# An attention and two expert layers on one core: the durations of the list scheduler set to those of a trace

## The chip, the cores and the metric

The kernel runs on one core of a Trainium2 chip. A core has four engines that compute: TensorE (PE in the profile; PEld is its weight loading), VectorE (DVE), ScalarE (ACT) and GpSimd (POOL). Each takes its instructions strictly in the order in which the program lists them. SyncE (SP) issues every DMA transfer of this kernel, also in order. The metric is the device time of one execution in microseconds (us).

## The reference

An attention for 4 batches of 8 heads (576 positions of 64 values, 32 packed queries) feeds a dense expert layer, and that feeds eight routed experts:

```python
p_packed = softmax(p @ k.T * scale) @ v          # 32 packed rows per head
x = softmax(q @ p_packed.T * scale) @ p_packed   # 576 rows per head -> [2304, 512]
h = x @ w_in                                     # w_in [512, 2048], float64
x = (h * clip(h + 3, 0, 6) / 6) @ w_out          # first layer
P = exp(x @ w_gate - max); 8 times: rows, then columns of P to a fixed sum
out = sum over e of P[:, e] * (relu(x @ w1[e]) @ w2[e])   # second layer, e = 0..7
```

The operands of the large products are split exactly into a high and a low part of twelve significant bits, and three passes (high by high, high by low, low by high) are summed in PSUM.

## The kernel before, in words

The program is not written in the order in which it runs. Every operation (one DVE instruction, one group of matmuls, one DMA) is first recorded with the engines that may do it, an assumed duration, the tiles that it reads and writes, and a priority. `Order.run` (line 95) then simulates the engines: again and again it takes, of the operations whose inputs are ready in the simulation, the one that can start first, ties going to the priority, and emits it. So the assumed durations decide both the order on each engine and, for operations with two possible engines, which engine does them. `alt` (line 299) lets POOL or DVE do a subtraction of two tiles, and DVE gets it only where it would end earlier than POOL by more than a margin `spare`; `copy` (line 289) chooses between ACT and DVE. `SYNC = 0.2` is added between an operation and whatever depends on it. The DMA's assumed time (`dma`, line 286) is the larger of 0.6 us and KiB / 350, and 2 us to land.

The durations come from four functions (lines 134 to 147): `t_dve`, `t_act`, `t_pool` and `t_pe`, each a fixed part and a part per column.

The work falls into these stages. In the attention, eight units of four heads each load k, q and v (lines 480, 497, 505), transpose and multiply them on PE (lines 527 to 772) and write tiles `a2`. In the same stretch the first float64 weights (tiles `raw`, line 381) are decoded on ACT, DVE and POOL into `w1f` (line 337) and `w2`. Then comes the first layer: `packed_weights` (matmuls of line 810), `layer1a` (lines 848 to 850, 288 columns) and `layer2a` (lines 885 to 887), 32 blocks in all. `third_phase` then frees memory, `operands` prepares the tokens of a pair of blocks for Winograd's form of Strassen's product (additions of line 936; high parts `xyh` and low parts `xyl`, lines 417 and 422), and the routing's 8 rounds run in small DVE operations. In the second layer a unit is one pair of token blocks with one group of 256 hidden units: seven products of 384 columns (lines 958 to 960, into `ph`), sums on DVE (line 967), relu on ACT (line 973), the split into `hsh` (ACT, line 417) and `hsl` (POOL or DVE, line 422), and six products of 512 columns (lines 1007 to 1009, into `po`), which DVE adds to `acc` (line 1031). There are 32 units for the first pair (a new group of weights for each), then 64 for the other two.

## Time and profile before

| what | value |
|---|---|
| three runs | 1975.92, 1979.96, 1982.13 us (median 1979.96) |
| the profiled execution, first to last instruction | 1972.3 us |
| PE busy in it | 1922.3 us, 97% |
| DVE, POOL, ACT busy | 1392.9, 1052.1, 874.1 us |
| last transposition of the attention | starts at 127.42 us |
| first layer ends, second begins | about 453.6 us |
| mean granted clock of PE | 0.996 |

The profile gives the span of the profiled execution, and no other time of that execution; the median of the runs is 7.7 us above the span, the fastest run 3.6 us.

A busy PE here means that a matmul is in flight. Since they overlap, a matmul's own length (338 ns for 384 columns) is about twice the distance from one to the next; the pace is read from counts in a stretch.

### The profile page before, as it was taken

The page shows a single profiled execution, that of the slowest core. Times are in us where ns is not written, and L with a number is a line of the kernel's source. Part 1 is how long each engine was busy: PE and PEld are TensorE (multiplying, and loading weights), DVE is VectorE, ACT ScalarE, POOL GpSimd, SP SyncE. Part 2 cuts the span into 40 slices and gives each one's busy share as a digit, 9 for nine tenths or more (in the row PEclk, how much of TensorE's full clock was granted, in tenths as well). Part 3 has the DMA queues.
Part 4 walks back from the last instruction along what each step waited for, and adds up shares of the span by engine and source line. Part 5 has one row for each costly group of instructions (what it writes and reads, how often), then busy time and mean ns, then how long its engine had stood idle before and what let it go on. Part 6 is the DMA issues. An engine that isn't in the chain of part 4 may idle for free.

```text
span 1972.3 us, 29636 instructions
## 1 busy us (share of the span) xinstructions
PE 1922.3 (97%) x10957; PEld 1733.2 (88%) x10957; DVE 1392.9 (71%) x2499; ACT 874.1 (44%) x1992; POOL 1052.1 (53%) x1045
## 2 busy tenths in 40 slices
PE   6999999998999999999999999999999999999998
PEld 4789989997888999999889899999999999999997
DVE  6885686437988777777866767667676676767665
ACT  6885775435354444444453334333333333333332
POOL 2454575326787766677744445454454544545442
PEclk9999999999999999999999999999999999999999
DMA  9921121001212221222301111110111111111102
GB/s 212 199 78 33 54 65 44 12 1 32 65 57 67 70 74 66 65 66 74 88 31 43 33 33 34 32 44 33 33 33 33 43 33 33 33 33 43 33 11 65
DMA packets 103553, 104.95 MB, mean 53 GB/s; under 512 B 42736, under 2 KB 78576, under 8 KB 103408
## 3 DMA queue, kind: packets, MB, share of 16 engines
q1 hardware_dynamic: 103408, 103.06, 19.0%
q8 instruction: 86, 1.41, 0.3%
q14 instruction: 59, 0.48, 0.1%
HBM read 98.32 MB, written 4.72 MB: 52 GB/s over the span
## 4 chain that ended last, share of the span: by engine, by line
PE 71%; DVE 4%; issue 1%; ACT 0%; ACTq 0%; DVEq 0%
PE po L1009 13%; PE po L1007 13%; PE po L1008 13%; PE ph L958 11%; PE ph L960 11%; PE ph L959 11%; DVE acc L1025 1%; DVE acc L1019 1%; DVE tmp L936 1%; DVE tmp L967 1%; DVE acc L1031 0%; DVE hsl L422 0%; DVE xyl L422 0%; DVE w1xl L422 0%; ACT tmp L973 0%
## 5 line engine op out<-in xcount | busy, mean ns | idle before, releaser
L422 POOL TENSOR_TENSOR hsl<-tmp,hsh 128x384 fp32r<-128x384 f32 (+1 forms) x503 | 505.1, 1019 | 541.0 <-ACT hsh L417 538.4
L1031 DVE SCALAR_TENSOR_TENSOR acc<-po,Pr,acc 128x512 f32<-128x512 f32 x504 | 373.6, 748 | 186.2 <-PE po L1009 184.8
L967 DVE TENSOR_TENSOR tmp<-ph,tmp 128x384 f32<-128x384 f32 x672 | 364.1, 554 | 165.9 <-PE ph L960 150.3
L1009 PE MATMUL po<-w2h,hsl 128*128 128x512 f32 x1152 | 449.1, 390 | 2.8 <-DVE hsl L422 2.8
L1007 PE MATMUL po<-w2h,hsh 128*128 128x512 f32 x1152 | 449.0, 390 | 1.3 <-ACT hsh L417 1.3
L1008 PE MATMUL po<-w2l,hsh 128*128 128x512 f32 x1152 | 448.8, 390 | 0.0
L973 ACT ACTIVATE tmp<-tmp 128x384 f32<-128x384 f32 x384 | 198.7, 521 | 460.1 <-DVE tmp L967 457.6
L958 PE MATMUL ph<-xyh,w1h 128*128 128x384 f32 x768 | 259.8, 338 | 7.9 <-DVE tmp L967 5.9
L959 PE MATMUL ph<-xyl,w1h 128*128 128x384 f32 x768 | 259.1, 337 | 2.3 <-DVE xyl L422 2.2
L1009 PEld LDWEIGHTS po<-w2h,hsl 128*128 128x128 f32 x1152 | 216.2, 188 | 49.8 <-DVE hsl L422 4.5
L960 PE MATMUL ph<-xyh,w1l 128*128 128x384 f32 x768 | 259.0, 337 | 0.0
L417 ACT ACTIVATE hsh<-tmp 128x384 fp32r<-128x384 f32 (+1 forms) x512 | 245.9, 498 | 22.4 <-DVE tmp L863 10.4
L1007 PEld LDWEIGHTS po<-w2h,hsh 128*128 128x128 f32 x1152 | 216.3, 188 | 43.1 <-ACT hsh L417 1.8
L1008 PEld LDWEIGHTS po<-w2l,hsh 128*128 128x128 f32 x1152 | 216.3, 188 | 41.5
L417 ACT ACTIVATE w2h<-raw 128x1024 fp32r<-128x1024 f32 x64 | 67.9, 1060 | 403.3 <-PE po L1009 394.1
L422 POOL TENSOR_TENSOR w2l<-raw,w2h 128x1024 fp32r<-128x1024 f32 x60 | 145.0, 2416 | 113.6 <-ACT w2h L417 113.6
L958 PE MATMUL ph<-xyh,w1xh 128*128 128x384 f32 x576 | 194.9, 338 | 0.5 <-ACT xyh L417 0.5
L959 PE MATMUL ph<-xyl,w1xh 128*128 128x384 f32 x576 | 194.6, 338 | 0.0
L960 PE MATMUL ph<-xyh,w1xl 128*128 128x384 f32 x576 | 194.4, 338 | 0.0
L958 PEld LDWEIGHTS ph<-xyh,w1h 128*128 128x128 f32 x768 | 144.9, 189 | 14.2 <-DVE tmp L967 4.2
L959 PEld LDWEIGHTS ph<-xyl,w1h 128*128 128x128 f32 x768 | 144.9, 189 | 6.4 <-DVE xyl L422 2.5
L960 PEld LDWEIGHTS ph<-xyh,w1l 128*128 128x128 f32 x768 | 145.0, 189 | 0.0
(186 smaller groups left out, 3242.1 us busy)
## 6 DMA issues: line engine op xcount, KB each, us to landing
raw<-in_moe_w_dram SPq DMA_DIRECT2D x128, 512.0 KB, 3.6
raw<-in_moe_w_in_dram SPq DMA_DIRECT2D x16, 512.0 KB, 3.9
raw<-in_moe_w_out_dram SPq DMA_DIRECT2D x16, 512.0 KB, 3.8
k<-in_k_dram SPq DMA_DIRECT2D x32, 144.0 KB, 5.5
q<-in_q_dram SPq DMA_DIRECT2D x32, 144.0 KB, 4.7
v<-in_v_dram SPq DMA_DIRECT2D x8, 576.0 KB, 6.7
out_dram<-acc SPq DMA_DIRECT2D x36, 128.0 KB, 2.4
p<-in_p_dram SPq DMA_DIRECT2D x1, 224.0 KB, 5.5
```

Of the source, the lines that this page charges most:

```text
L417: t_act(n), lambda: nc.scalar.activation(dst(w.t[0]), src(), AF.Copy),
L422: lambda e: e.tensor_tensor(dst(w.t[1]), src(), as_f32(dst(w.t[0])), ALU.subtract),
L936: lambda e, s=s, i0=i0, i1=i1, how=how: e.tensor_tensor(s.t, i0(), i1(), how),
L958: nc.tensor.matmul(out, wh[:, at + c, :], bh[:, c, :], start=(c == 0), stop=False)
L959: nc.tensor.matmul(out, wh[:, at + c, :], bl[:, c, :], start=False, stop=False)
L960: nc.tensor.matmul(out, wl[:, at + c, :], bh[:, c, :], start=False, stop=(c == 1))
L967: t_dve(n), lambda: nc.vector.tensor_tensor(dst.t, ps.t[:, :n], u.t, ALU.add),
L973: act(t_act(n), lambda: nc.scalar.activation(c.t, c.t, AF.Relu), writes=[c], **quick)
L1007: nc.tensor.matmul(ps.t, hh[:, f, ts], wh[:, f, :], start=(f == 0), stop=False)
L1008: nc.tensor.matmul(ps.t, hh[:, f, ts], wl[:, f, :], start=False, stop=False)
L1009: nc.tensor.matmul(ps.t, hl[:, f, ts], wh[:, f, :], start=False, stop=(f == NFC - 1))
L1031: lambda row=row, share=share, ps=ps: nc.vector.scalar_tensor_tensor(row(), ps.t, share(), row(), ALU.mult, ALU.add),
```

## The change

Only the four functions change their numbers; comments and docstrings are emptied too, so that no line moves. The operations, their arithmetic and the tiles are the same. Each assumed duration grows: 384 columns on DVE from 0.465 to 0.55 us, on ACT from 0.415 to 0.51, on POOL from 0.976 to 1.053, one matmul of 384 columns on PE from 0.163 to 0.173.

```diff
 def t_dve(n, fast=False):
-    return 0.065 + n / (1920.0 if fast else 960.0)
+    return 0.15 + n / (1920.0 if fast else 960.0)
 
 def t_act(n, psum=False):
-    return (0.05 if psum else 0.095) + n / 1200.0
+    return (0.165 if psum else 0.19) + n / 1200.0
 
 def t_pool(n):
-    return 0.15 + n / 465.0
+    return 0.2 + n / 450.0
 
 def t_pe(n, count=1):
-    return count * (0.003 + n / 2400.0)
+    return count * (0.0133 + n / 2400.0)
```

What the built program makes of it is shown at three places. The first is SP at the end of the attention's loads: k, q and v are the attention's inputs, `raw` a piece of 512 KB of the first layer's weights. Before:

```order
L497 DMA q_1257<-in_q_dram 64x9x64 x4
L505 DMA v_1332<-in_v_dram 96x4x384
L480 DMA k_0_1369<-in_k_dram 96x6x64
L381 DMA raw_1389<-in_moe_w_out_dram 128x512
L480 DMA k_0_1369<-in_k_dram 96x6x64
L480 DMA k_0_1433<-in_k_dram 96x6x64
L381 DMA raw_1437<-in_moe_w_out_dram 128x512
L480 DMA k_0_1433<-in_k_dram 96x6x64
L497 DMA q_1483<-in_q_dram 64x9x64 x4
L505 DMA v_1621<-in_v_dram 96x4x384
```

And now:

```order
L497 DMA q_1197<-in_q_dram 64x9x64 x4
L480 DMA k_0_1256<-in_k_dram 96x6x64 x2
L480 DMA k_0_1279<-in_k_dram 96x6x64 x2
L505 DMA v_1307<-in_v_dram 96x4x384
L381 DMA raw_1377<-in_moe_w_in_dram 128x2x256
L497 DMA q_1412<-in_q_dram 64x9x64 x4
L505 DMA v_1459<-in_v_dram 96x4x384
L381 DMA raw_1489<-in_moe_w_in_dram 128x2x256
L381 DMA raw_1682<-in_moe_w_out_dram 128x512
L381 DMA raw_1737<-in_moe_w_out_dram 128x512
```

Two pieces of weights stood between the loads of the last unit before; now one does, and others come behind the last v. In the whole list 12 pieces stand ahead of the last v before, and 9 now.

PE follows that: ahead of the attention's last transposition (line 772) it had 216 matmuls of the first layer (84 of lines 848 to 850 and 132 of lines 885 to 887), and has 138 now (54 and 84). From its row 467 to its row 2543, which is the end of the first layer and a little beyond, PE's order is the same as before; row 491 is the matmul of line 810 with which the last of the first four batches of weights is put to use.

The second place is DVE and PE between the layers. DVE there makes the first pair's operands; `w2l` is a low part of weights, of 1024 columns. DVE before, from the first addition on:

```order
L936 TENSOR_TENSOR tmp_6078<-acc_0_1608 128x384
L936 TENSOR_TENSOR tmp_6092<-acc_0_1254,acc_0_1608 128x384
L936 TENSOR_TENSOR tmp_6103<-tmp_6078,acc_0_1254 128x384
L422 TENSOR_TENSOR xyl_6090<-acc_0_1254,xyh_6089 128x384
L422 TENSOR_TENSOR w2l_6072<-raw_4617,w2h_6071 128x1024
L422 TENSOR_TENSOR xyl_6113<-acc_0_1608,xyh_6112 128x384
L422 TENSOR_TENSOR xyl_6080<-tmp_6078,xyh_6079 128x384
```

DVE now:

```order
L936 TENSOR_TENSOR tmp_6078<-acc_0_1789 128x384
L936 TENSOR_TENSOR tmp_6096<-tmp_6082,acc_0_1563 128x384
L936 TENSOR_TENSOR tmp_6101<-tmp_6078,acc_0_1563 128x384
L422 TENSOR_TENSOR w2l_6072<-raw_4717,w2h_6071 128x1024
L422 TENSOR_TENSOR xyl_6106<-acc_0_1563,xyh_6105 128x384 x2
L422 TENSOR_TENSOR xyl_6112<-acc_0_1789,xyh_6111 128x384
L422 TENSOR_TENSOR xyl_6080<-tmp_6078,xyh_6079 128x384
```

PE's first product there, before:

```order
L958 MATMUL ph_6116<-xyh_6089,w1h_4412 128x384
L959 MATMUL ph_6116<-xyl_6090,w1h_4412 128x384
L960 MATMUL ph_6116<-xyh_6089,w1l_4413 128x384
L958 MATMUL ph_6116<-xyh_6089,w1h_4412 128x384
L959 MATMUL ph_6116<-xyl_6090,w1h_4412 128x384
L960 MATMUL ph_6116<-xyh_6089,w1l_4413 128x384
```

and now:

```order
L958 MATMUL ph_6122<-xyh_6105,w1h_4518 128x384
L959 MATMUL ph_6122<-xyl_6106,w1h_4518 128x384
L960 MATMUL ph_6122<-xyh_6105,w1l_4519 128x384
L958 MATMUL ph_6122<-xyh_6105,w1h_4518 128x384
L959 MATMUL ph_6122<-xyl_6106,w1h_4518 128x384
L960 MATMUL ph_6122<-xyh_6105,w1l_4519 128x384
```

The `w2l` stood behind one `xyl` half, the one that PE's first product reads (its other half is POOL's); now it stands ahead of both halves of the `xyl` that PE's first product reads, and both are DVE's.

The third place is DVE in the second layer's steady part, over the end of one unit and the start of the next. Before:

```order
L967 TENSOR_TENSOR tmp_14359<-ph_14435,tmp_14359 128x384
L967 TENSOR_TENSOR tmp_14451<-ph_14435,tmp_14393 128x384
L967 TENSOR_TENSOR tmp_14393<-ph_14443,tmp_14393 128x384
L967 TENSOR_TENSOR tmp_14359<-ph_14453,tmp_14359 128x384
L294 COPY tmp_14484<-ph_14465 128x384
L967 TENSOR_TENSOR tmp_14495<-ph_14476,tmp_14484 128x384
L422 TENSOR_TENSOR w1l_14498<-raw_14261,w1h_14497 128x512
L967 TENSOR_TENSOR tmp_14484<-ph_14488,tmp_14484 128x384
L967 TENSOR_TENSOR tmp_14523<-ph_14502,tmp_14484 128x384
```

and now:

```order
L967 TENSOR_TENSOR tmp_15204<-ph_15281,tmp_15204 128x384
L967 TENSOR_TENSOR tmp_15297<-ph_15281,tmp_15238 128x384
L967 TENSOR_TENSOR tmp_15238<-ph_15289,tmp_15238 128x384
L967 TENSOR_TENSOR tmp_15204<-ph_15299,tmp_15204 128x384
L294 COPY tmp_15332<-ph_15312 128x384
L422 TENSOR_TENSOR hsl_15322<-tmp_15238,hsh_15321 128x384
L967 TENSOR_TENSOR tmp_15345<-ph_15324,tmp_15332 128x384
L967 TENSOR_TENSOR tmp_15332<-ph_15337,tmp_15332 128x384
```

DVE now makes one `hsl` of each unit (95 in all against 7 before; POOL makes 289 against 377), put between the sums of the next unit. In exchange POOL makes most low parts of the weights: 184 of the 192 `w1xl` of 256 columns against 128, and 60 of the 64 `w1l` of 512 columns against 6. PE's order changes with it in about half of the units: the six products of 512 columns begin behind the third product of the next unit instead of the fourth.

## Rows read from the trace of the kernel before

**Rows 1.** The page: busy time and share of each engine.

```profile
PE 1922.3 (97%) x10957; PEld 1733.2 (88%) x10957; DVE 1392.9 (71%) x2499; ACT 874.1 (44%) x1992; POOL 1052.1 (53%) x1045
```

**Rows 2.** Busy time by stage; columns are named in its first line.

```profile
core 0: us, PE busy (x) PEld busy (x) DVE busy (x) ACT busy (x) POOL busy (x), PEclk, DMA share, GB/s
0.00:127.40 127.40, 104.31 (x1079) 84.63 (x1080) 103.78 (x284) 99.02 (x262) 54.30 (x58) 1.00 0.86 176
127.40:146.58 19.18, 17.81 (x128) 15.51 (x126) 14.51 (x32) 16.63 (x43) 9.89 (x11) 1.00 0.29 85
146.58:453.60 307.02, 302.59 (x2235) 279.37 (x2235) 182.17 (x426) 163.93 (x420) 154.23 (x193) 0.99 0.11 34
453.60:600.00 146.40, 136.16 (x665) 120.02 (x664) 129.15 (x235) 71.99 (x159) 109.31 (x102) 0.97 0.18 58
600.00:975.00 375.00, 375.00 (x1892) 340.18 (x1891) 285.15 (x468) 172.69 (x372) 268.52 (x247) 1.00 0.22 69
975.00:990.00 15.00, 11.14 (x57) 9.63 (x56) 14.76 (x20) 7.24 (x15) 12.38 (x12) 1.00 0.49 131
1110.00:1955.00 845.00, 845.00 (x4264) 767.11 (x4263) 573.38 (x893) 291.85 (x619) 387.00 (x374) 1.00 0.11 33
```

**Rows 3.** PE's longest wait, in the view of waits: total us, times, longest.

```profile
PE tp L527 <- DMA k<-in_k_dram: 9.4, 4, 7.9
```

**Rows 4.** The same view by stretch, the first 105 us.

```profile
0.00:105.00 105.00, 83.48 (x861) 65.80 (x863) 82.65 (x234) 81.60 (x214) 40.13 (x45) 1.00 0.97 195
```

**Rows 5.** SP's issues in order of time: start, length, line, transfer.

```profile
90.14 0.35 SPq L381 DMA_DIRECT2D raw<-in_moe_w_out_dram  x1
102.61 0.34 SPq L505 DMA_DIRECT2D v<-in_v_dram  x1
```

**Rows 6.** PE in order of time at two marks.

```profile
127.42 0.27 PE L772 MATMUL tp<-ident,e 128*64 128x128 f32 x1
...
146.58 0.44 PE L810 MATMUL ph<-w1f,ppT 128*64 128x256 f32 x2
```

**Rows 7.** Groups by line and shape, whole span: busy us, mean ns.

```profile
L422 POOL TENSOR_TENSOR hsl<-tmp,hsh 128x384 fp32r<-128x384 f32 x377 | 399.8, 1075 | 402.9 <-ACT hsh L417 400.8 <-issue 1.5
L967 DVE TENSOR_TENSOR tmp<-ph,tmp 128x384 f32<-128x384 f32 x672 | 364.1, 554 | 165.9 <-PE ph L960 150.3 <-POOL hsl L422 0.9
L422 DVE TENSOR_TENSOR hsl<-tmp,hsh 128x384 fp32r<-128x384 f32 x7 | 8.7, 1239 | 1.9 <-ACT hsh L417 1.9
```

**Rows 8.** One DVE group in 600 to 950, then in 1200 to 1900.

```profile
L422 DVE TENSOR_TENSOR w1l<-raw,w1h 128x512 fp32r<-128x512 f32 x23 | 15.8, 687 | 1.4 <-ACT w1h L417 1.3
...
L422 DVE TENSOR_TENSOR w1l<-raw,w1h 128x512 fp32r<-128x512 f32 x23 | 35.5, 1544 | 0.0
```

**Rows 9.** All engines in order of time, between the two layers.

```profile
456.08 1.36 DVE L936 TENSOR_TENSOR tmp<-tmp,acc 128x384 f32<-128x384 f32 x1
457.36 1.35 DVE L422 TENSOR_TENSOR xyl<-acc,xyh 128x384 fp32r<-128x384 f32 x1
458.63 2.03 DVE L422 TENSOR_TENSOR w2l<-raw,w2h 128x1024 fp32r<-128x1024 f32 x1
458.76 0.69 PE L959 MATMUL ph<-xyl,w1h 128*128 128x384 f32 x1 [2.18 <-DVE xyl L422]
464.83 0.49 PE L958 MATMUL ph<-xyh,w1h 128*128 128x384 f32 x1 [2.04 <-ACT tmp L293]
```

**Rows 10.** All engines, the end of one block in the second layer.

```profile
1307.85 0.34 PE L960 MATMUL ph<-xyh,w1l 128*128 128x384 f32 x1
1308.23 0.56 DVE L967 TENSOR_TENSOR tmp<-ph,tmp 128x384 f32<-128x384 f32 x1 [0.40 <-PE ph L960]
1308.24 1.10 ACT L973 ACTIVATE tmp<-tmp 128x384 f32<-128x384 f32 x2
1309.25 0.92 ACT L417 ACTIVATE hsh<-tmp 128x384 fp32r<-128x384 f32 x2
1309.84 2.00 POOL L422 TENSOR_TENSOR hsl<-tmp,hsh 128x384 fp32r<-128x384 f32 x2 [0.41 <-ACT hsh L417]
```

## The prediction

> **What bounds the kernel now.** I read the page's engine table first, then the busy time by stage, then PE's waits, and last the timelines of the two places where PE stands still. PE is busy 1922.3 of 1972.3 us [rows 1], so all that another order can win is in the 50 us in which it is not, and in the small matmuls of the attention. By stage [rows 2] the reader is to see where these 50 us are: 23.1 in the attention (127.40 - 104.31), 1.4 just behind it, 4.4 in the first layer, 10.2 between 453.6 and 600 us, where the layers meet, 3.9 at 975 to 990 us, where the second pass starts; the other 7 us are mostly at the end. From 600 to 975 and from 1110 to 1955 PE has no idle time at all: 1892 matmuls in 375.00 us are 0.198 us each. These 1220 us can't get shorter by an order of the same matmuls; they can only get longer.
>
> What bounds the attention is another matter. In the first 105 us the DMA engines are busy for 0.97 of the time and move 195 GB/s [rows 4], which is 20.5 MB; DVE, ACT and PE are each busy about 80%. PE's largest wait for a transfer is one of 7.9 us at the start, and only 1.5 us come after it [rows 3], so the transfers do not show as PE's waits; they show as a stage that can't be quicker than its bytes.
>
> **The attention's loads and the first layer's matmuls.** This is the largest move. Of the pieces of 512 KB (0.524 MB) 12 stand ahead of the last v before, and 9 now. Three pieces less are 1.57 MB, at 195 GB/s [rows 4] 8.1 us. The last v is issued at 102.61 us, behind a piece issued at 90.14 [rows 5], and the attention's last transposition runs at 127.42 [rows 6], 24.8 us later. If the unit's chain stays as long, the last transposition comes at 127.4 - 8.1 = 119.3 us. Against this, PE has done less of the first layer by then: 138 matmuls of 288 columns instead of 216. The 78 that are left come later at the first layer's pace: 2235 matmuls in 302.59 us of busy time [rows 2] are 0.135 us each, so 10.5 us. At PE's row 491, from where both programs have the same PE order to the end of the layer, the trace reads 146.58 us [rows 6]; now it should be 146.6 - 8.1 + 10.5 = 149.0, a loss of 2.4 us. Bounds: if compute and not bytes sets the end of the attention, and it does not move, the loss is 10.5; if the new order also takes out half of the 15.2 us of PE's idle time behind its first wait (23.1 - 7.9), the result is 2.4 - 7.6, a gain of 5.2. I take +2.4, because the row on the DMA engines is the one that is nearest to full. The deferred pieces are needed at PE's row 463, which is 162 rows (22 us at 0.135) behind the last transposition and so 46 us behind the last v; no row prices their decoding in the new order, and I count no stall for it.
>
> **The first layer from row 491 on.** PE's order is the same to its end. Its 4.4 us of idle time stay: 0, within 2 either way.
>
> **Between the layers.** Before, PE's first product reads a low part of which POOL made one half and DVE the other; DVE's `xyl` stands behind three additions, the last of which ends at 457.4, and PE takes up the low half at 458.76 [rows 9]. Then DVE does `w2l`, 2.03 us. Now the `w2l` stands first, and both halves come behind it at 1.35 us each (the length of DVE's `xyl` there): 457.4 + 2.0 + 2 x 1.35 = 462.1, against 458.76, so PE's first product ends 3.4 us later. Of this a part comes back: before, PE waited 2.04 us for its third product at 464.83 [rows 9], since a sum's place was not free; now the first two products have been waiting for DVE, and the next operands are ready while they run. 3.4 - 2.0 = 1.4; with the routing's rounds and the second pair's operands behind it, where the order moves in small things that I can't price one by one, I take +1. Bounds: +3.4 and, if half of the stage's 10.2 us goes, -5.
>
> **The second layer's steady part.** DVE now makes one `hsl` of each unit, at 1.239 us by the only seven that DVE did (POOL: 1.075), where the new table says 0.55. The table is right for DVE's sums out of PSUM, 0.554 [rows 7], and wrong for a DVE operation on two tiles of SBUF while POOL works. The same `w1l` of 512 columns took 687 ns in one stretch and 1544 in another [rows 8]. What does a late `hsl` cost? The chain at a unit's end: PE starts the last matmul of the last product at 1307.85, DVE's sum starts at 1308.23, two relus end at 1309.34, two high parts at 1310.17, the two low parts on POOL at 1311.84 [rows 10]: 3.6 us from the sum. Now six products of 512 columns begin three products of 384 columns behind the unit's last one, 3 x 6 x 0.173 = 3.1 us, not 4.2 (0.173 is the new table's figure; with 36 matmuls of 512 columns at 0.227 the 78 of a unit give 15.4 us, which is 78 x 0.198, as the trace has it). But the low part that is late belongs to the second of those products or to its last matmuls, 1.4 us and more later, so it is needed 4.5 us behind the last product and is there after 3.6 to 4.3. The DVE operation also holds up two sums of the next unit by some 0.7 us; DVE has idle time in every unit and four PSUM places cover four products. I count 0. Bounds: 0, since PE had no idle time to give back, and 0.69 us (1.239 - 0.55) in each of the 88 added ones, 61 us, if every one stood on PE's path.
>
> The trace shows how two such operations meet, and a page bears on it. DVE's 1544 ns come where POOL is busy with `hsl` [rows 8]. The Trainium skill's page "SBUF — State Buffer", section "Who interferes with whom", says that a VectorE instruction with two inputs in SBUF contends with a GpSimd instruction that reads SBUF, and that the one that comes second waits for the whole of the first. The trace agrees: 1544 is 687 and some 0.86 of waiting. By that rule this part of the change is worse than its table believes; it is the third rival's mechanism below, and gives no other sum than the bounds above.
>
> **The tail and the second pass's start.** The last products stand in nearly the same order; 0, within 1.5.
>
> **The sum.** 2.4 + 0 + 1 + 0 + 0 = +3.4 us against the profiled execution: 1972.3 + 3.4 = 1975.7 us. The median of the runs is 7.7 us above that span, so the time to be measured is 1983.4, say 1983. With 0.3% (5.9 us) as the least that a measurement of this kernel tells from no change, this is no change: 1974.0 to 1985.9 counts as the same.
>
> **The rivals.**
> - *True durations make a better order (faster).* The waits of PE outside the steady part are 15.2 + 10.2 + 3.9 = 29.3 us [rows 2, 3]; an order made with durations that are 10 to 25% longer leaves fewer instructions in front of others that are ready. If half of the 29.3 goes, the time is 1980 - 14.6 = 1965. For it: these are just the stages where DVE is the busiest, and its durations were short by 0.085 us each. Against it: the two places that I worked out do not get better, and the lengths at which DVE and POOL collide (1.35 and 2.03 us) are in neither table.
> - *The attention ends no earlier (slower).* Then only the 10.5 us of first-layer work that was put off remain, and with the 1 us between the layers the time is 1980 + 11.5 = 1991.5. Place: from the last transposition to PE's row 491. It decides if the last transposition comes later than about 122 us. For it: DVE and ACT are busy 82% and 78% of the stage [rows 2]. Against it: both have less to do by then, as the put-off matmuls carry their relus and splits with them, and the DMA engines are at 0.97.
> - *DVE's added `hsl` comes too late (slower).* From a lateness of about 1 us (the slack above) PE waits in every unit. At 0.3 us in each of 88 units that is 26 us: 2006, with 61 us as the end.
> - *The table does not do what its change says.* The DMA's assumed cost and the contended lengths stay as they were, so the durations are still not those of the trace. This is no case of its own: it is why I expect little.
>
> **How the numbers follow.** The forecast, +3.4 with its own range 1976 to 1988: 0.48. Faster by a better order: 0.22. The attention ends no earlier: 0.2. Late `hsl`: 0.1. The range that should hold 8 in 10 goes from 1967, near the first rival's time, to 1996, beyond the second's; the third's is left out. Faster by over 0.3% (under 1974): the first rival, with a little less for its weak half and a little of the forecast's low end, 0.23. Slower (over 1985.9): the second and third rival with a fifth of the forecast's case, 0.37. Same: 0.40.
>
> **What would show it.** In the new trace: the last v issued near 94 us and the last transposition near 119 (right), or both where they were (second rival); PE's row 491, the eighth group of line 810, near 149 us; PE's wait for `xyl` between the layers 3 us longer, and its wait at the third product gone; no idle time of PE in the steady part, with DVE's `hsl` at 0.7 to 1.3 us. The prediction is wrong if row 491 comes before 143 or after 155 us, if PE's busy share of the steady part falls under 1, or if the stage between the layers gains or loses more than 6 us.

## The result, and the profile after

The kernel after takes 1989.67 us (median of 4 runs, 1986.33 to 1992.17), the kernel before 1979.05 us (4 runs, 1975.92 to 1982.13). The ratio is 1.0062 with an interval of 1.0048 to 1.0077: slower by 0.6%. That is inside the predicted range of 1967 to 1996, but it is not the forecast's case, which was no change at 1983.

Between the two profiled executions the gap is larger: the spans are 1972.3 and 1989.0 us, 16.7 us apart, where the medians are 10.6 apart. The profiled execution of after took 1990.77 us, 1.8 more than its span and 1.1 more than its median. With the same 1.8, that of before took some 1974.1 us (an estimate), 4.9 less than its median; 4.9 and 1.1 make up the difference. The engine table of the kernel after, the line that answers to [rows 1]:

```profile
PE 1929.0 (97%) x10957; PEld 1740.9 (88%) x10957; DVE 1366.1 (69%) x2470; ACT 874.8 (44%) x1983; POOL 1072.2 (54%) x1083
```

The 16.7 us have two parts. PE has the same 10957 matmuls and is busy 6.7 us longer with them (1929.0 - 1922.3), and it is idle 10.0 us longer (60.0 against 50.0). Since the matmuls are the same, the first part is their pace: the mean granted clock is 0.991 after and 0.996 before. Busy time by stage, kernel after, with the columns of [rows 2]; the stages are cut at the same events, except the second pass's start, which comes some 15 us later, and the steady part of that pass:

```profile
0.00:123.20 123.20, 97.73 (x1001) 78.71 (x1002) 92.72 (x265) 85.53 (x225) 43.12 (x49) 0.94 0.85 170
123.20:162.04 38.84, 29.85 (x205) 27.50 (x203) 31.96 (x49) 29.70 (x70) 23.69 (x21) 0.96 0.23 69
162.04:465.60 303.56, 302.40 (x2235) 279.34 (x2235) 178.72 (x425) 165.46 (x425) 160.58 (x200) 0.99 0.12 36
465.60:600.00 134.40, 123.15 (x598) 108.12 (x597) 115.13 (x210) 63.77 (x139) 94.22 (x93) 0.96 0.18 55
990.00:1005.00 15.00, 13.85 (x73) 12.53 (x72) 14.90 (x22) 9.21 (x20) 14.46 (x14) 1.00 0.50 122
1126.00:1971.00 845.00, 845.00 (x4264) 767.12 (x4263) 554.30 (x898) 291.20 (x620) 383.66 (x370) 1.00 0.11 33
```

The row to look at is the second. Behind the attention's last transposition PE needed 19.18 us for 128 matmuls to its row 491 before, and stood still for 1.4 of them. Now it needs 38.84 us for 205, and stands still for 9.0. Of the 19.7 us that this stretch is longer, 12.0 are PE's busy time (77 more matmuls, some of them at a lower clock) and 7.6 its waits. The last row shows the steady second layer untouched: 845.00 of 845.00 us.

To see where the spans part, I took the start of PE's n-th matmul in both traces and subtracted. Both run 10957 matmuls, and from PE row 491 to the second layer in the same order. In us, each kernel against the profiled execution of before (the experiments in the other lines are told below):

| kernel | 1300th (159.5 before) | 3400th (447.7) | 4500th (679.6) | 10900th (1953.3) |
|---|---|---|---|---|
| after | +17.0 | +11.9 | +19.8 | +16.5 |
| e1 new ahead of layer 2 | +17.0 | +11.9 | +11.3 | +11.3 |
| e2 new in layer 2 | +5.0 | +4.5 | +12.4 | +8.2 |
| e3 urgency 8.4 | +12.4 | +7.2 | +14.9 | +10.7 |
| e4 DMA cost KiB/200 | +27.4 | +27.9 | +31.3 | +32.0 |
| e5 old, pieces late | +16.0 | +16.0 | +16.0 | +16.0 |
| e6 new, v behind pieces | +16.6 | +11.4 | +18.9 | +13.9 |
| e7 new, w2l held | +18.6 | +13.5 | +13.7 | +10.5 |
| e8 old and new mixed | +3.2 | -1.9 | +3.1 | -0.1 |
| e9 mixed, w2l held | +2.5 | -2.5 | -1.9 | -5.1 |
| e10 old on ScalarE | +3.7 | +4.0 | +4.5 | +1.2 |
| e11 handicap 0.1 | +10.7 | +7.6 | +6.4 | +2.4 |
| e12 new on ScalarE | +10.0 | +14.2 | +13.8 | +14.0 |

So the kernel after loses 17.0 us up to the 1300th matmul, wins back 5.1 in the first layer, loses 7.8 between the layers and wins back 3.3 at the second pass's start.

Four marks of the loss, the kernel after. First SP, columns as in [rows 5]:

```profile
66.08 0.35 SPq L381 DMA_DIRECT2D raw<-in_moe_w_out_dram  x1
...
68.62 0.57 SPq L381 DMA_DIRECT2D raw<-in_moe_w_out_dram  x1
...
96.67 0.87 SPq L505 DMA_DIRECT2D v<-in_v_dram  x1
98.44 0.40 SPq L381 DMA_DIRECT2D raw<-in_moe_w_in_dram  x1
113.81 2.82 SPq L381 DMA_DIRECT2D raw<-in_moe_w_out_dram  x2
129.85 5.26 SPq L381 DMA_DIRECT2D raw<-in_moe_w_in_dram  x2
142.80 5.62 SPq L381 DMA_DIRECT2D raw<-in_moe_w_out_dram  x2
```

And the same pieces in the kernel before:

```profile
43.91 0.56 SPq L381 DMA_DIRECT2D raw<-in_moe_w_out_dram  x1
...
55.16 0.57 SPq L381 DMA_DIRECT2D raw<-in_moe_w_out_dram  x1
...
104.79 6.18 SPq L381 DMA_DIRECT2D raw<-in_moe_w_in_dram  x2
123.21 6.41 SPq L381 DMA_DIRECT2D raw<-in_moe_w_out_dram  x2
```

The last v is indeed issued 6 us earlier (96.67 against 102.61). But the seventh piece of weights is issued at 66.08 us instead of 43.91, and the last two of the sixteen from 142.80 instead of 123.21. They come in pairs every 13 to 16 us, and the DMA engines are busy only 0.23 of that stretch: the bytes don't hold them up, the two places of `raw` do. Why the seventh comes late stands in the timeline of ACT and DVE: it waits for the place of the fifth piece. Two steps of the fifth piece's decoding, kernel after:

```profile
49.88 0.62 ACT L360 ACTIVATE m_early<-m_early 128x512 f32<-128x512 f32 x1
...
60.12 0.43 DVE L362 TENSOR_SCALAR m_early<-m_early 128x512 uint32<-128x512 uint32 x1
```

and in the kernel before:

```profile
35.92 0.65 ACT L360 ACTIVATE m_early<-m_early 128x512 f32<-128x512 f32 x1
...
36.69 0.42 DVE L362 TENSOR_SCALAR m_early<-m_early 128x512 uint32<-128x512 uint32 x1
```

Before, DVE takes line 362 0.12 us behind ScalarE's end. After, line 362 stands behind the attention's reductions and copies, DVE works through them without a gap, and the decoding rests for 9.6 us (60.12 - 49.88 - 0.62). This is the longest rest, but not the only one: ScalarE's line 360 already runs 14.0 us later than before (49.88 against 35.92). The third mark is PE, columns as in [rows 6]:

```profile
123.22 0.27 PE L772 MATMUL tp<-ident,e 128*64 128x128 f32 x1
...
154.91 0.40 PE L848 MATMUL ph<-a2h,pwh 128*128 128x288 f32 x1 [2.47 <-DVE pwl L830]
...
162.04 1.55 PE L810 MATMUL ph<-w1f,ppT 128*64 128x256 f32 x6 [1.90 <-DVE tmp L863]
```

The last transposition is earlier (123.22 against 127.42), row 491 later (162.04 against 146.58). What PE waits for there, kernel after, 100 to 165 us, columns as in [rows 3]:

```profile
PE ph L848 <- DVE tmp L863: 4.6, 3, 3.2
PE ph L848 <- DVE pwl L830: 2.5, 1, 2.5
PE ph L810 <- DVE tmp L863: 1.9, 1, 1.9
```

In the kernel before the same three are 2.0, 0.2 and 0.3 us. So PE waits for DVE's results and not directly for a tile of weights. But on DVE these results stand behind the decoding of the late pieces, as the `pwl` of the 2.5 us does:

```profile
152.44 1.35 DVE L353 TENSOR_SCALAR m_early<-m_early 128x512 f32<-128x512 f32 x1 [0.45 <-ACT m_early L342]
...
154.17 1.34 DVE L830 TENSOR_TENSOR pwl<-ph,pwh 128x512 fp32r<-128x512 f32 x2
```

The fourth mark is the clock, in the columns of [rows 2], four stretches around these waits:

```profile
149.00:155.19 6.19, 3.72 (x30) 2.67 (x29) 4.93 (x8) 4.42 (x10) 1.28 (x1) 1.00 0.37 101
155.19:158.60 3.41, 3.41 (x16) 3.35 (x16) 1.89 (x4) 1.76 (x5) 2.58 (x2) 0.50 0.36 130
158.60:162.01 3.41, 1.55 (x10) 1.13 (x9) 3.41 (x6) 2.54 (x7) 2.00 (x2) 1.00 0.01 2
162.01:165.42 3.41, 3.38 (x14) 2.24 (x15) 2.62 (x5) 2.30 (x7) 2.44 (x3) 0.50 0.50 154
```

PE stood still 2.5 of 6.2 us, and then 1.9 of 3.4; behind each the granted clock is 0.50 (1.2 instead of 2.4 GHz) for 3.41 us, in which PE does 14 to 16 matmuls instead of about 25. Such a wait thus costs its own length and up to 1.7 us more. Not every wait does: behind the longest one of this stretch the clock stays at 1.00 (132.80 to 149.00 us).

```profile
132.80 0.40 PE L848 MATMUL ph<-a2h,pwh 128*128 128x288 f32 x1 [3.21 <-DVE tmp L863]
```

Between the layers, kernel after, columns as in [rows 9], DVE and PE:

```profile
466.75 2.64 DVE L936 TENSOR_TENSOR tmp<-tmp,acc 128x384 f32<-128x384 f32 x2
...
469.31 2.02 DVE L422 TENSOR_TENSOR w2l<-raw,w2h 128x1024 fp32r<-128x1024 f32 x1
...
471.25 3.09 DVE L422 TENSOR_TENSOR xyl<-acc,xyh 128x384 fp32r<-128x384 f32 x3
...
472.65 0.69 PE L959 MATMUL ph<-xyl,w1h 128*128 128x384 f32 x1 [4.88 <-DVE xyl L422]
```

`w2l` stands ahead of both `xyl`, as the order said, and PE's wait is 4.88 us instead of 2.18. The delay of 5.3 us is gone by the 3475th matmul (+11.1, after +17.2 at the 3450th and +11.9 at the 3400th): the wait of 2.04 us at the third product [rows 9] and the half clock behind it are not there. The stage's loss comes later. PE's waits of the kernel after from 460 to 640 us (columns as in [rows 3]):

```profile
PE ph L958 <- DVE tmp L967: 5.3, 2, 3.5
PE ph L959 <- DVE xyl L422: 4.9, 1, 4.9
PE ph L1137 <- DVE cs L1132: 4.4, 4, 2.3
```

The same waits in the kernel before, from 450 to 640 us:

```profile
PE ph L958 <- DVE tmp L967: 3.0, 3, 2.3
PE ph L959 <- DVE xyl L422: 2.2, 1, 2.2
PE ph L1137 <- DVE cs L1132: 1.6, 2, 1.0
```

### The profile page after: what moved, and what is told of

The parts are those of the page before. It is cut to its first block, busy times and chain, and to the rows that moved or that the text cites. A ratio compares the mean times of both kernels' runs of the same rounds, so it can differ in the third digit from the quotient of the medians.

```text
span 1989.0 us, 29571 instructions
## 1 busy us (share of the span) xinstructions
PE 1929.0 (97%) x10957; PEld 1740.9 (88%) x10957; DVE 1366.1 (69%) x2470; ACT 874.8 (44%) x1983; POOL 1072.2 (54%) x1083
## 4 chain that ended last, share of the span: by engine, by line
PE 87%; DVE 6%; DMA 2%; POOL 1%; issue 1%; ACT 1%; SPq 1%; POOLq 0%; DVEq 0%; ACTq 0%
PE po L1009 12%; PE po L1008 12%; PE po L1007 12%; PE ph L958 11%; PE ph L959 11%; PE ph L960 11%; PE po L885 3%; PE po L886 3%; PE po L887 3%; PE ph L848 2%; PE ph L850 1%; PE ph L849 1%; PE ph L810 1%; DMA k<-in_k_dram 1%; DVE tmp L967 1%
## 5 line engine op out<-in xcount | busy, mean ns | idle before, releaser
L422 POOL TENSOR_TENSOR hsl<-tmp,hsh 128x384 fp32r<-128x384 f32 (+1 forms) x415 | 402.7, 975 | 316.3 <-ACT hsh L417 297.5
L422 POOL TENSOR_TENSOR w1xl<-m,w1xh 128x256 fp32r<-128x256 f32 x184 | 153.8, 849 | 283.9 <-ACT w1xh L417 273.7
L417 ACT ACTIVATE w1xh<-m 128x256 fp32r<-128x256 f32 x192 | 72.3, 408 | 354.3 <-PE ph L959 339.5
L958 PEld LDWEIGHTS ph<-xyh,w1h 128*128 128x128 f32 x768 | 145.2, 189 | 10.5 <-DVE tmp L967 7.2
```

Source lines behind the costliest of these rows:

```text
L417: t_act(n), lambda: nc.scalar.activation(dst(w.t[0]), src(), AF.Copy),
L422: lambda e: e.tensor_tensor(dst(w.t[1]), src(), as_f32(dst(w.t[0])), ALU.subtract),
L958: nc.tensor.matmul(out, wh[:, at + c, :], bh[:, c, :], start=(c == 0), stop=False)
```

## Experiments

Twelve kernels ran, each beside the kernel before. Ratios are to its runs on the same chip, in brackets the interval. In all of them 16 early pieces of weights (512 KB each) are loaded. Marks of the head, in us (the kernel after in the second line):

| kernel | 7th piece issued | 16th | last transposition | 1300th matmul | 1300th - 16th |
|---|---|---|---|---|---|
| before | 43.9 | 129.3 | 127.4 | 159.5 | 30.2 |
| after | 66.1 | 148.1 | 123.2 | 176.5 | 28.4 |
| e1 | 65.7 | 148.3 | 123.4 | 176.5 | 28.2 |
| e2 | 45.0 | 134.3 | 132.4 | 164.5 | 30.2 |
| e3 | 41.7 | 142.3 | 146.4 | 171.9 | 29.6 |
| e4 | 40.7 | 149.0 | 175.7 | 186.9 | 37.9 |
| e5 | 44.1 | 146.6 | 126.2 | 175.5 | 28.9 |
| e6 | 66.2 | 148.3 | 138.2 | 176.1 | 27.8 |
| e7 | 66.1 | 152.0 | 124.6 | 178.1 | 26.1 |
| e8 | 44.5 | 131.9 | 126.0 | 162.7 | 30.8 |
| e9 | 43.8 | 131.1 | 125.3 | 162.0 | 30.9 |
| e10 | 46.2 | 134.7 | 132.9 | 163.2 | 28.5 |
| e11 | 51.6 | 138.2 | 130.0 | 170.2 | 32.0 |
| e12 | 51.1 | 140.4 | 122.7 | 169.5 | 29.1 |

**e1 and e2: the change cut in two at the second layer.** The four functions take new or old numbers by a flag, which is turned over where the second layer's operations are made. e1 (e2 has True and False exchanged):

```diff
+NEW = [True]
-    return 0.065 + n / (1920.0 if fast else 960.0)
+    return (0.15 if NEW[0] else 0.065) + n / (1920.0 if fast else 960.0)
...
-        order.op([("", 0.0, third_phase)], after=order.all[begun:])
+        NEW[0] = False; order.op([("", 0.0, third_phase)], after=order.all[begun:])
```

> The new durations for everything ahead of the second layer, the old ones from there: its order on all engines is that of the kernel after to the end of the first layer, and that of the kernel before from there. Theory A (the loss is made of places that stand by themselves: +17.0 us up to the 1300th matmul, -5.7 in the rest of the first layer, +7.8 between the layers, -3.2 at the second pass's start): 1300th matmul at 176.5 us as in the kernel after (159.5 before), and a time 11 to 13 us over the kernel before, in spans. Rival (what is lost between the layers comes out of the head, because its late pieces push the rest): the full 16 us over the kernel before.

> The opposite: old durations ahead of the second layer, new ones in it. Theory A: 1300th matmul at 159.5 us, 4 to 6 us slower than the kernel before, all of it between 453 and 640 us and a part back at the second pass's start; no idle time of PE in the steady parts. Rival (the head is the whole cause): within 1.5 us of the kernel before.

Measured: e1 1.0051 (1.0038 to 1.0065), e2 1.0015 (1.0006 to 1.0024); together 1.0066, the whole change's 1.0062. By medians e2 is 3.5 us slower, a little under the 4 to 6 expected. The parts stand by themselves: theory A was right in this, and the rivals (all in the head, or a loss that grows) fall. e2 showed one thing not expected. Its order up to the second layer is the kernel before's, and yet its 1300th matmul comes 5.0 us later. 3.3 of these arise between the 300th and the 450th matmul, and PE's waits up to 70 us of e2 show where:

```profile
PE tp L527 <- DMA k<-in_k_dram: 13.2, 5, 7.9
```

It was 9.4 us in the profiled execution of before [rows 3]. Against e2 the kernel after loses 12.0 us in the head, against before 17.0. Which of the two starts is the usual one, these traces don't settle. e5, e8 and e9 begin with the old order too, and their 450th matmul comes only 0.3 to 1.0 us later than before's, where e2's comes 4.4 later; and e2's profiled execution is the slowest of its eleven (1982.47 us, median 1980.27). So e2's start may as well be the unlucky one, and the new order's share of the head lies between 12 and 17 us. From the 1000th to the 1300th matmul the loss is 11.5 us against either.

**e3 and e4: more pieces ahead of the last v.**

```diff
-        return (9.4, 9.4, 13.4, 14.4, 100, 100, 100, 100)[gg]
+        return (8.4, 8.4, 13.4, 14.4, 100, 100, 100, 100)[gg]
```

```diff
-        return order.op([("SP", max(0.6, kib / 350.0), fn)], lat=2.0, **kw)
+        return order.op([("SP", max(0.6, kib / 200.0), fn)], lat=2.0, **kw)
```

The scheduler puts a handicap of 0.2 us (`PATIENCE`) on an operation (not on a load) whose urgency lies between 9 and 20 with a fraction over 0.3, or from 100 on. With 8.4 these two groups fall out of it, and no other operation's urgency lies between 8.4 and 9.9; so what e3 takes away is their handicap.

> The kernel after with one number changed: the first two groups' weights get urgency 8.4 instead of 9.4. From the first layer's PE row 467 on all engines' order is that of the kernel after; ahead of the last v stand 14 of the 16 early pieces of weights instead of 9, and 308 of the first layer's matmuls ahead of the last transposition instead of 158. Theory A (each early piece that is put behind the last v costs 6 to 7 us of loading and decoding, two pieces every 13 to 16 us, during which PE starves): the waits of PE behind the attention go, and the 1300th matmul comes at 156 to 163 us (kernel after 176.5), although the last transposition comes later than in the kernel after; time within 5 us of e2's difference, that is about 4 us over the kernel before. Rival B (the new durations make a worse order of the vector operations in the attention whatever stands where): the 1300th matmul stays over 170 us.

> The kernel after with the one duration that the change left as it was also set near the trace's: a transfer's assumed cost is KiB/200 instead of KiB/350 us (512 KB cost 2.6 instead of 1.46 us). All 16 early pieces then stand ahead of the last v, and 368 first-layer matmuls ahead of the last transposition. Theory A: 1300th matmul at 155 to 165 us, 10 to 18 us faster than the kernel after. Rival C (an order by truer numbers isn't better; what matters is what happens to stand where): no better than the kernel after, 1300th matmul at 170 us or more.

Measured: e3 1.0043 (1.003 to 1.0056), 1300th matmul at 171.9 us; e4 1.0146 (1.0132 to 1.016), 186.9 us. e3's head lies nearer to rival B, and e4 is rival C's case. Theory A falls in the form that counts pieces ahead of the last v. Early pieces are bought with a late attention: its last transposition moves from 123.2 to 146.4 and 175.7 us. e4 also shows that a truer number alone (512 KB at 2.6 us) needn't make a better order: it is the slowest of all.

**e5 and e6: the pieces moved in the scheduler, the durations left.** e5 is the kernel before with each piece after the ninth made to wait for the last v's load; e6 the kernel after with the last v's load made to wait for pieces ten to twelve (`loads` and `last_v` collect these operations).

```diff
+        for o in loads[9:]:
+            if o in order.open: order.open.remove(o)
+            o.wait.add(last_v[0]); last_v[0].after.append(o)
```

```diff
+        order.open.remove(last_v[0])
+        for o in loads[9:12]:
+            last_v[0].wait.add(o); o.after.append(last_v[0])
```

> The kernel before (old durations everywhere) with one rule more for the scheduler: no early piece of weights after the ninth goes ahead of the last v. So 9 pieces stand ahead of it instead of 12, as in the kernel after; all engines' orders are the kernel before's up to about PE row 180 and from row 467 on, and 244 of the first layer's matmuls stand ahead of the last transposition (before 236, after 158). Theory A', which is what is left of theory A after e3 and e4 fell (seven pieces behind the last v are loaded and decoded through two places at about 6.6 us each, two every 13 to 16 us by the trace of after, and PE starves at the end of that chain): the 1300th matmul comes 8 to 13 us later than in e2, whose order up to there is the kernel before's, so at 172 to 178 us against 164.5; the time 7 to 12 us over the kernel before. Rival B (the new durations' order of the vector operations around the attention costs it, not the pieces): within 3 us of e2's 164.5 us, and the time that of the kernel before.

> The opposite: the kernel after (new durations everywhere), with the last v held behind the twelfth early piece in the scheduler. 12 pieces stand ahead of it, and 254 first-layer matmuls ahead of the last transposition; the orders are the kernel after's up to PE row 225 and from row 467 on. Theory A': the last transposition later than in the kernel after (130 to 135 us against 123.2), but the 1300th matmul earlier, at 162 to 168 us against 176.5; the time 8 to 13 us under the kernel after, so 2 to 6 us over the kernel before. Rival B: 1300th matmul at 174 us or later.

Measured: e5 1.0074 (1.006 to 1.0088), 1300th matmul at 175.5 us; e6 1.0061 (1.0049 to 1.0074), 176.1. e5 agrees with A': old durations and late pieces give the same loss in the head, and since nothing is won back later its time lies even above the range given. PE's waits of e5 from 100 to 165 us name the missing weights, where in the kernel after the last wait is for DVE's `tmp` and `pwl` behind the decoding; the loss is alike, the wait that ends last is not:

```profile
PE ph L810 <- DVE w1f L337: 6.7, 2, 5.5
PE po L885 <- ACT w2oh L417: 4.1, 1, 4.1
```

e6 missed: 176.1 us where A' expected 162 to 168. The table of marks says why. Its pieces are issued when they were in the kernel after (the sixteenth at 148.3 and 148.1 us); only the v got later. A piece goes out when a place of `raw` comes free, so in the kernel after its turn on SP follows from the decoding. (Where its turn alone is put off, as in e5, the loss comes as well.) In the table the 1300th matmul follows the sixteenth piece by 26.1 to 32.0 us in all kernels but e4, where the attention itself ends late. This is theory D, for e10 to e12. e5 and e6 also lose this much without putting matmuls off: 228 and 234 of the first layer's stand ahead of the last transposition, where the kernel before has 216 and the kernel after 138.

**e7: the `w2l` held.** In the kernel after, the low part of the second group's output weights waits for the two low parts of the first operand.

```diff
+                if turn == 101 + G1:
+                    for d in (order.all[n0 + 1], order.all[n0 + 3]):
+                        order.all[-1].wait.add(d); d.after.append(order.all[-1])
```

> The kernel after with the low part of the second layer's second group of output weights (DVE's w2l of 1024 columns, 1.94 us, which stands ahead of both low parts of the tokens' first operand) held behind them. Orders are the kernel after's to the end of the first layer and again from early in the second layer. Theory W (this w2l is what the stage between the layers loses by): PE's wait of 4.9 us for xyl falls to 2 to 3 us, and the stage's loss (from 11.9 us at the 3400th matmul to 19.8 at the 4500th, against the kernel before) falls from 7.8 to 3 to 5 us. Rival V (the first product's delay is given back at the third product anyway, and the stage's loss comes from its later waits, for cs and tmp, 2.3 us and more each, and from the half clock granted after them): the loss stays 6.5 us or more.

Measured: 1.004 (1.0028 to 1.0053). The stage's loss from the 3400th to the 4500th matmul falls from 7.8 us to 0.2, further than theory W said. But PE's waits of e7 from 460 to 640 us show that the price wasn't the first product:

```profile
PE ph L958 <- DVE tmp L967: 5.2, 3, 4.6
PE ph L959 <- DVE xyl L422: 2.7, 2, 2.2
PE ph L958 <- ACT tmp L293: 2.2, 1, 2.2
...
PE ph L1137 <- DVE cs L1132: 0.4, 1, 0.4
```

The wait for `xyl` falls to 2.2 us at the first product, the one at the third product (for ScalarE's copy) is back, and the 4.4 us for the routing's `cs` are gone. Rival V was right that the first delay is given back, and wrong that holding `w2l` changes nothing: the scheduler places the routing anew behind it. Which of the moved instructions frees `cs` stays open.

**e8 and e9: new durations only where the kernel after gained.** e8 has the new numbers from the first layer's units to its end and in the second pass; e9 from the first layer on, with e7's rule.

```diff
-        begun = len(order.all)
+        begun = len(order.all); NEW[0] = True
...
         for ps in passes:
+            NEW[0] = len(ps) > 1
```

> Old durations for the attention, the early weights and the second layer's first pass; new ones for the first layer and the second layer's second pass, the two places where the kernel after gained on the kernel before (5.7 us around the 2100th matmul, 3.2 at the second pass's start, which e2 shows too and e1 does not). 12 early pieces ahead of the last v, 200 first-layer matmuls ahead of the last transposition. If these gains belong to the new order there: 1300th matmul within 3 us of e2's 164.5, and 3 to 8 us faster than the kernel before. Rival (the first gain belongs to when things meet, not to the order): only the 3.2 us of the second pass, so 1973 to 1977.

> e8's first half (old durations for the attention and the early weights, new ones for the first layer) and e7's second half (new durations in the whole second layer, the w2l held behind the first operand's low parts). Theory W, on which the held w2l is the whole loss between the layers: 1300th matmul near e8's 162.7 us, no loss between the 3400th and 4500th matmul against the kernel before (within 1.5 us), 3 us gained at the second pass's start, so 3 to 6 us faster than the kernel before and 1 to 4 faster than e8. Rival (e7's +0.2 us there was how the waits happened to fall): 4 us or more lost in that stage.

Measured: e8 0.9988 (0.998 to 0.9997), 1974.1 us; e9 0.9974 (0.9964 to 0.9983), 1970.8 us (9 runs) against 1975.73, faster than both kernels. The first layer's gain belongs to the new durations there: e8 and e9 win 5.1 and 4.9 us from the 1300th to the 3400th matmul, the kernel after 5.1, e2 0.5 and e5 nothing. It is these lines of the kernel before that are gone, a wait and (columns of [rows 2]) a stretch at half clock:

```profile
280.53 1.78 PE L810 MATMUL ph<-w1f,ppT 128*64 128x256 f32 x8 [2.21 <-DVE tmp L863]
```

```profile
280.77:284.18 3.41, 3.41 (x16) 2.42 (x13) 3.00 (x8) 3.41 (x11) 3.15 (x4) 0.50 0.00 0
```

By its time e8 (2.6 us faster) would stand with the rival; that is because it loses 4.9 us between the layers, which e9 does not (+0.6). e8 has the old durations between the layers, so a loss there is not the new durations' alone; e1, e5 and e12, old there too, have none. e9 came as theory W had it. The engine table of e9:

```profile
PE 1922.6 (98%) x10957; PEld 1732.4 (88%) x10957; DVE 1353.9 (69%) x2465; ACT 875.4 (44%) x1993; POOL 1064.3 (54%) x1078
```

Of its span of 1969.0 us PE is idle 46.4, 3.6 less than before, at the same busy time.

**e10, e11, e12: whose duration puts the decoding behind.** e10 takes ScalarE's old numbers up to the end of the first layer, new ones else, and e9's second layer; e12 is its mirror image, with the old second layer. e11 halves the handicap that the scheduler gives to early decoding (and to that of all later weights).

```diff
-    return (0.165 if psum else 0.19) + n / 1200.0
+    return ((0.165 if psum else 0.19) if NEW[0] is True else 0.05 if psum else 0.095) + n / 1200.0
```

```diff
-PATIENCE = 0.2
+PATIENCE = 0.1
```

> New durations everywhere but on ScalarE up to the end of the first layer, where they are the old ones; second layer as in e9. 12 early pieces ahead of the last v, 254 first-layer matmuls ahead of the last transposition. Theory D (the head's loss is that the decoding of the early pieces falls behind: the seventh piece is issued at 66 us in the kernel after and at 44 before, the sixteenth at 148 and 129, and the 1300th matmul follows the sixteenth piece by 28 to 30 us in nearly all runs so far), with ScalarE's longer durations as what puts the decoding behind: seventh piece at 42 to 52 us, sixteenth at 125 to 138, 1300th matmul at 154 to 167. If DVE's and PE's durations do it: seventh piece over 58, sixteenth over 142, 1300th matmul over 170.

> The kernel after with the scheduler's handicap on early decoding and on the later matmuls at 0.1 us instead of 0.2 (PATIENCE). 11 pieces ahead of the last v, 200 first-layer matmuls ahead of the last transposition. Theory D: the decoding is held back less, the seventh piece is issued at 50 to 62 us, the sixteenth at 132 to 144, the 1300th matmul 28 to 31 us behind it, at 160 to 174; so 2 to 12 us faster than the kernel after. Rival: as late as in the kernel after (176.5 us), or the 1300th matmul no longer 28 to 31 us behind the sixteenth piece.

> The old durations, with ScalarE's new ones up to the end of the first layer. 10 pieces ahead of the last v and 158 first-layer matmuls ahead of the last transposition (as many matmuls as in the kernel after). If ScalarE's durations alone put the decoding behind (theory D as in e10): sixteenth piece at 140 us or later, 1300th matmul 170 or later, 6 us or more slower than the kernel before. If it takes the other engines' as well: sixteenth piece at 128 to 138, 1300th matmul at 157 to 167, time within 4 us of the kernel before.

Measured: e10 1.0018 (1.0009 to 1.0027), e11 1.0019 (1.001 to 1.0027), e12 1.0061 (1.0048 to 1.0074). e10's marks are all inside theory D's: without ScalarE's new numbers the decoding keeps its pace, and 13.4 of the kernel after's 17.0 us are gone. SP's issues of the seventh piece and of the last pair in e10:

```profile
46.21 0.51 SPq L381 DMA_DIRECT2D raw<-in_moe_w_out_dram  x1
...
129.63 5.40 SPq L381 DMA_DIRECT2D raw<-in_moe_w_out_dram  x2
```

ScalarE's numbers alone (e12) do some two fifths of it: the 1300th matmul comes 5.0 us later than in e2, in the kernel after 12.0. Its sixteenth piece (140.4 us) and its time (12.2 us slower) fall in the first of its two cases and its 1300th matmul (169.5, against 170 or later) just misses it; nothing falls in the second. So ScalarE's numbers are needed for the loss (e10) and make less than half of it alone. e11 lies within its ranges for the marks, and half the handicap gives back 6.3 us of the head. But its 1300th matmul comes 32.0 us behind the sixteenth piece, not 28 to 31, which its rival had as a condition; the rule of theory D is a rough one. In the first layer itself, from the 1300th to the 3400th matmul, e10 loses 0.3 us and e12 4.2: neither ScalarE's new numbers alone nor the others' alone bring the gain of 5 us. All together bring it in the kernel after, e1, e3 and e6 to e9; e11 wins 3.1, and e4 loses 0.5.

## Why the prediction was right or wrong

The time lies in the range and the forecast's mechanism failed. Two of the three signs by which the prediction called itself wrong have come: row 491 at 162.04 us (later than 155), and 7.8 us lost between the layers (more than 6). That the range holds is luck in part: the terms were off by +14.6 (against before), -5.1, +6.8 and -3.3 us, which partly cancel, and its upper end came from a rival with another mechanism. The prediction also added the whole 7.7 us between before's span and the median of its runs; 1.8 of them are time outside the span, and only the rest tells how quick that execution was.

*The attention's loads and the first layer's matmuls: the step that failed.* Predicted +2.4, bounds -5.2 and +10.5; measured +15.5 at row 491 and +17.0 at the 1300th matmul, of which 12 to 17 are the order's. The attention did end earlier: by 9.2 us against e2 and by 4.2 against before (predicted 8.1). At the 1000th matmul the kernel after is level with e2 (+5.5 and +5.0). What failed is the last sentence: "no row prices their decoding in the new order, and I count no stall for it". From the 1000th to the 1300th matmul PE loses 11.5 us, 6.1 of them idle (9.0 against 2.9) and the rest in longer busy time at a lower clock (0.94 against 1.00). I priced a deferred piece at its bytes, 2.7 us each (8.1 / 3), where the loads come in pairs every 13 to 16 us, 6.5 to 8 a piece, because two places are held until the decoding is through. The bound of +10.5 was no bound: it left the stall out too. And the number of pieces ahead of the last v was a symptom (e6), not the lever; the lever was the decoding, which rests behind the attention's work on ScalarE and DVE, 9.6 us in one place.

*The second rival.* By its own criterion (last transposition later than 122 us; it was 123.2) it should have decided, and its 1991.5 us lies near the 1989.67 measured. But its mechanism is wrong: the attention did end earlier, by 4.2 us or more, and the loss came behind it; and e5 and e6 lose as much with the put-off matmuls back in their place. That its time is right is luck.

*The first layer from row 491 on.* Predicted 0 within 2; a gain of 5.1, shown by e8 and e9 to belong to the new durations there (all of them together, by e10 and e12). I took "the same PE order" for "the same waits", but DVE's order had changed.

*Between the layers.* Predicted +1, bounds -5 and +3.4; measured +7.8, outside. The worked-out part was right in kind: the first product was later (5.3 us, predicted 3.4) and the third's wait went with it (all 5.3 came back). What I called small things that I can't price, the routing behind it, was the loss, with waits of up to 2.3 us for `cs` and 3.5 for `tmp` and half clock behind them.

*The second layer's steady part.* 0 as predicted, and the third rival is refuted: 845.00 of 845.00 us busy. But not for the reason given. The added `hsl` does not take 1.239 us; in the steady second pass, 55 of them:

```profile
L422 DVE TENSOR_TENSOR hsl<-tmp,hsh 128x384 fp32r<-128x384 f32 x55 | 30.9, 561 | 0.6 <-ACT hsh L417 0.6
```

The table's 0.55 us was right here. Each of the seven before [rows 7] began while an operation of POOL was running (the one at 490.03 us 0.08 us behind POOL's `hsl`, and it took 1357 ns); these mostly meet only the end of one: the one at 1264.48 us begins 0.09 us before POOL's `hsl` ends, and POOL's next begins at 1264.94. The Trainium skill's page "SBUF — State Buffer", section "Who interferes with whom", makes contention a matter of two instructions meeting; this row agrees, at 561 ns. The reading of the `w1l` needs a correction: the 687 ns were not without POOL, and [rows 8] doesn't show POOL at all. In the first stretch POOL's `hsl` ran beside the `w1l` too, but it came second (`w1l` at 702.50, `hsl` at 702.54 us) and took 1.52 us instead of 1.02. Where the `w1l` took 1544 ns, it came second itself (`hsl` at 1372.63, `w1l` at 1372.65).

*Tail and second pass's start.* Predicted 0 within 1.5; a gain of 3.3, in every kernel with new durations in the second pass (from the 5900th to the 6100th matmul 3.3 in the kernel after, 2.2 in e8, 1.7 in e4) and in none of e1, e5 and e12.

*That truer durations make a better order* was the first rival, and it is half true: true in the first layer (of the whole table) and in the second pass, false in the attention and, without the held `w2l`, between the layers.

## What to carry to other kernels

When a reordering puts off loads that go through few places, price each by the time its place is held (landing and decoding), read from the distance of two issues in the trace, and not by its bytes; then look for who needs the last one. A list scheduler's durations can gain in one stage and lose in the next, and a handicap of 0.2 us decides as much as they do (e3, e11). So change them stage by stage and keep the stages that gain: here this, with one operation held, was worth 0.26% where the whole table cost 0.62%. And profile the same order twice before you explain 5 us in a stage that transfers bound.

## What the runs showed of the hardware

A wait of PE of 2 us can cost more than itself: behind most such waits of the kernel after the granted clock is 0.50 for 3.41 us or twice that. It is not so behind each: none follows the wait of 3.21 us at 132.80 us, nor one of 2.21 us at 981.32 us in the kernel before.

Of a VectorE and a GpSimd instruction that read two tiles of SBUF each, the one that came 0.02 to 0.04 us later took longer: `w1l` on DVE 1544 ns instead of 687, `hsl` on POOL 1.52 us instead of 1.02.

By the mean granted clock the kernel after lacks 17.9 us of full speed (0.009 x 1989.0) and the kernel before 7.9 (0.004 x 1972.3); the difference of 10.0 us is an upper limit of what the clock adds to the slowdown, since PE partly waits meanwhile, and PE's busy time gives 6.7.
